# A verdict in five steps, two split loads and a new written order in a gated attention and SoLU kernel

## The chip, the core and the metric

The kernel runs on one core of a Trainium2 chip. Its engines work side by side, each through its own queue in order: TensorE (PE, with its weight loads shown apart as PEld), VectorE (DVE), ScalarE (ACT), GpSimd (POOL) and SyncE (SP), which here issues nearly all DMA transfers. The metric is the time of one execution on the device in microseconds (us). A profile is one execution as the hardware profiler saw it; its span runs from the first to the last instruction.

## The reference

Two blocks follow each other. The first is a gated linear recurrence over 768 time steps, for 4 batches and 8 heads of 48 elements; the gate is complex and its magnitude is clipped:

```python
mag = np.sqrt(a_re * a_re + a_im * a_im)
scale = np.minimum(mag, 0.999) / (mag + 1e-06)
a_re_n, a_im_n = (a_re * scale, a_im * scale)
...
for t in range(S):
    new_re = ar * S_re - ai * S_im
    new_im = ar * S_im + ai * S_re
    S_re, S_im = (new_re + kv, new_im)
    y[:, :, t] = np.einsum('bhd,bhde->bhe', q[:, :, t], S_re)
```

Here kv is the outer product of k and v at step t. Its result, seen as 3072 tokens of 384 values, goes through the second block, with w_in of 384 x 1024 and w_out of 1024 x 384:

```python
h = x @ w_in
e = np.exp(h - h_max)
sm = e / (np.sum(e, axis=-1, keepdims=True) + 1e-09)
solu = h * sm
ln = (solu - mu) / np.sqrt(var + 1e-06) * g_ln
return (ln @ w_out).astype(np.float32)
```

## The kernel before

Time is cut into 6 pieces of 128 steps. A group is one such piece for two batches (12 groups), a chunk is one piece of one batch (24 chunks, two to a group).

For each group the gates are prepared: loads of a_re and a_im (`load_ar`, `load_ai`), then a chain of element operations on ACT and DVE in turn (`inverse`, `ratio`, `sure`, `tangent`, `square`, `secant`, `fourth`, `size`, `eps`, `lnm`) that ends in the logarithm of the magnitude. `total0` and `total1` are its running sums over time, as products on PE with a triangular matrix (L838, one for each batch); `grow` and `decay` take exponentials of them, `angle` and `phase` do the same for the argument, `nearest`, `part`, `cos` and `sin` give the rotations. `trig` and `exp` are loads of ACT's function tables (L933, L936). `qs` and `ks` scale q and k. For group 0 alone the chain is cut in two halves, batch 0 (steps ending in a) and batch 1 (ending in b), though a_re and a_im arrive as one tile for both.

For each chunk `k2` and `q2` build doubled rows on DVE (L947), which are transposed, for chunks 0 and 1 on PE (`qt`, `kt`, copied by ACT as `qT`, `kT`), for the others by DVE and four DMAs (`kqb`, `kqt0`; L956, L961). `score0` and `score1` are products (L1001), `mask0` multiplies by the causal mask on DVE (L1006), `values` is the product with v and the carried state (L1034), `carry` and `add` renew the state (L1042).

The second block follows chunk by chunk: `turned_x` (ACT copy), `up0` and `up1` (PE, f_h, L1075), `exp0` (ACT, f_z), `solu0` (DVE), a transpose (`zt`, `zT` by PE and ACT for chunks 0, 1, 2 and 23, `blocks` and `away` by DVE and four DMAs for the others), `centred`, `spread` and `norm` for the variance, `down0` and `down1` (PE, f_o, L1152), `scale` (ACT, L1156) into f_ot, a pool of two buffers, and `store` (L1161).

The weights are stored as 64-bit numbers. `fetch` brings one of 14 pieces (pieces 0 to 5 of w_in, 6 to 13 of w_out) into a pool of six buffers (f_raw), `raised` (ACT, L736) and `convert` (DVE, three operations, L742 to L746) turn it into 32-bit numbers. `mean`, `meansum` and `centre` take a weighted column mean from w_out. The kernel relies on its inputs lying in certain ranges: extremes are noted along the way (`seen`, `rows`, `sums`), and near the end the 14 pieces are fetched again (`again`) and examined (`inspect`, L749, into `least`). The verdict (L1180 to L1195) counts all of these into one flag. All queues load the flag (L1261), and if it is not zero a slower general program runs (L1262); with these inputs it does not.

The order of all instructions is written out by hand in the list `ORDER`: steps are issued in its order, each engine works through its own share, and waits follow from the data. A step such as `up0:22` is `up0` of chunk 22, for prep steps the number is that of the group, for weight steps that of the piece. Behind the list the code calls the verdict:

```python
for s in ORDER.split():
    nm, i = s.split(":")
    go(nm, int(i))
go("verdict", 0)
```

A buffer of a pool goes to the next tile once the readers of its old tile are done.

Of the kernel before, what the change touches and what calls it, by code (L numbers as in the profile page):

```python
# [19 lines left out]
P = 128  # L20
# [495 lines left out]
load_ar:0 inverseb:0 load_ai:0 ratiob:0 inversea:0 ratioa:0 sureb:0 surea:0 fetch:10 raised:10 tangentb:0 squareb:0  # L516
load_q:0 fetch:1 tangenta:0 squarea:0 secantb:0 secanta:0 sizeb:0 fourthb:0 sizea:0 epsb:0 convert:10 fetch:0 epsa:0
load_k:0 lnmb:0 fetch:3 raised:0 lnma:0 total1:0 fourtha:0 total0:0 decay1:0 grow1:0 convert:0 grow0:0 fetch:4
decay0:0 ks0:0 fetch:11 trig:0 anglea:0 raised:3 load_vr:0 load_ai:1 qs1:0 phase0:0 angleb:0 load_ar:1 nearest0:0
phase1:0 qs0:0 ks1:0 fetch:2 raised:1 convert:3 part0:0 nearest1:0 sina:0 cosa:0 fetch:5 gain:0 convert:1 raised:11  # L520
part1:0 convert:11 raised:4 load_v:0 cosb:0 sinb:0 q2:0 k2:0 fetch:9 fetch:13 q2:1 exp:0 qt1:0 qT1:0 qt0:0 kt1:0 qT0:0
convert:4 inverse:1 kT1:0 kt0:0 score1:0 kT0:0 score0:0 k2:1 onward:0 ratio:1 mask0:0 qt1:1 raised:5 values:0 kt1:1
sure:1 raised:2 qT1:1 fetch:6 tangent:1 square:1 fetch:8 last:0 turned_x:0 kt0:1 convert:2 secant:1 raised:13 kT1:1
convert:5 size:1 convert:13 raised:9 fetch:7 up0:0 eps:1 turn_ends:0 fourth:1 up1:0 raised:6 tot:0 kT0:1 convert:9
lnm:1 exp0:0 fetch:12 raised:7 convert:6 total0:1 carry:1 load_vr:1 total1:1 score1:1 convert:7 grow0:1 decay0:1
solu0:0 decay1:1 grow1:1 trig:1 angle:1 load_q:1 raised:12 load_k:1 qt0:1 ks0:1 phase0:1 qT0:1 phase1:1 nearest1:1
add:1 carry:0 load_ai:2 load_ar:2 nearest0:1 score0:1 convert:12 part1:1 raised:8 part0:1 convert:8 mean:0 mean:4
mean:2 mean:3 qs0:1 sin:1 zt1:0 cos:1 mean:1 mean:6 mask0:1 mean:5 q2:2 k2:2 mean:7 add:0 meansum:0 kqb:2 load_q:2
exp:1 load_q:3 centre:2 values:1 zT1:0 inverse:2 ratio:2 kqt0:2 centre:7 onward:1 turned_x:1 sure:2 centred:0 zt0:0
qs1:1 up1:1 zT0:0 up0:1 last:1 centre:0 tangent:2 score0:2 square:2 score1:2 centre:3 centre:4 secant:2 centre:5 ks1:1  # L530
exp0:1 size:2 load_k:2 centre:1 centre:6 q2:3 eps:2 load_v:1 fourth:2 k2:3 lnm:2 kqb:3 down0:0 turn_ends:1 tot:1
total0:2 spread:0 total1:2 grow1:2 grow0:2 mask0:2 decay0:2 decay1:2 trig:2 solu0:1 down1:0 angle:2 load_ar:3 values:2
kqt0:3 norm:0 scale:0 on:2 load_vr:2 load_ai:3 zt0:1 turned_x:2 zt1:1 carry:2 qs0:2 zT0:1 zT1:1 centred:1 phase0:2
qs1:2 phase1:2 ks1:2 score1:3 load_v:2 score0:3 up1:2 nearest0:2 nearest1:2 ks0:2 part0:2 load_v:4 part1:2 sin:2 add:2
cos:2 up0:2 mask0:3 q2:4 k2:4 exp:2 values:3 down0:1 kqb:4 inverse:3 spread:1 down1:1 turned_x:3 ratio:3 exp0:2 sure:3
solu0:2 kqt0:4 tangent:3 square:3 zt1:2 zt0:2 norm:1 last:2 zT1:2 zT0:2 up1:3 secant:3 size:3 carry:3 load_k:3
score1:4 load_ar:4 k2:5 eps:3 up0:3 scale:1 q2:5 centred:2 exp0:3 lnm:3 score0:4 total0:3 total1:3 kqb:5 load_q:4
fourth:3 grow1:3 decay0:3 kqt0:5 add:3 grow0:3 decay1:3 onward:2 mask0:4 down0:2 store:0 trig:3 solu0:3 angle:3 on:3
centred:3 down1:2 spread:2 values:4 blocks:3 turn_ends:2 last:3 tot:2 turned_x:4 load_ai:4 phase0:3 phase1:3 carry:4
qs0:3 nearest0:3 ks1:3 nearest1:3 ks0:3 part1:3 away:3 store:1 score1:5 norm:2 part0:3 sin:3 cos:3 scale:2 score0:5  # L540
qs1:3 exp:3 up1:4 inverse:4 mask0:5 add:4 up0:4 exp0:4 k2:6 spread:3 q2:6 kqb:6 values:5 ratio:4 load_v:3 sure:4
turned_x:5 solu0:4 down0:3 tangent:4 again:12 turn_ends:3 blocks:4 down1:3 norm:3 square:4 carry:5 kqt0:6 up0:5 up1:5
secant:4 load_vr:3 away:4 q2:7 score1:6 scale:3 size:4 k2:7 eps:4 lnm:4 score0:6 tot:3 total0:4 kqb:7 fourth:4 store:3
total1:4 down0:4 add:5 grow0:4 decay1:4 onward:3 centred:4 exp0:5 spread:4 down1:4 decay0:4 grow1:4 trig:4 load_k:4
mask0:6 angle:4 kqt0:7 values:6 solu0:5 blocks:5 turned_x:6 last:4 on:4 store:2 phase0:4 away:5 phase1:4 load_ar:5
score0:7 carry:6 nearest1:4 ks0:4 nearest0:4 norm:4 qs0:4 centred:5 part1:4 score1:7 part0:4 sin:4 cos:4 add:6 scale:4
# [51 lines left out]
centred:22 store:20 blocks:22 up0:23 scale:21 up1:23 spread:22 away:22 again:2 inspect:5 exp0:23 norm:22 inspect:3  # L598
down0:22 again:0 down1:22 solu0:23 inspect:9 centred:23 scale:22 again:11 again:6 zt0:23 zT0:23 inspect:0 inspect:6
zt1:23 again:4 again:8 store:22 spread:23 inspect:2 store:21 down0:23 norm:23 inspect:8 again:1 zT1:23 down1:23  # L600
inspect:11 inspect:4 scale:23 store:23 inspect:1
"""


# [690 lines left out]
```

## Time and profile before

| | |
|---|---|
| median of 4 runs | 433.65 us (433.12 to 434.98) |
| the profiled execution's own time | 434.3 us |
| its span | 432.4 us |
| mean granted TensorE clock | 0.985 |
| PE, DVE, ACT, POOL busy | 89%, 78%, 67%, 13% of the span |
| bytes read from HBM, written | 38.87 MB, 4.72 MB |

The span is shorter than the time, since it leaves out what lies before the first and behind the last instruction. Busy shares are averages over stages with different limits: the opening (the first 85 us or so), a long middle in which the work of one group repeats, and the end.

The DMA work of SP shows in the list of issues (out<-in, engine, count, size, median us from issue to landing):

```profile
f_kqT<-f_kb SPq DMA_DIRECT2D x88, 192.0 KB, 3.4
f_zT<-f_zb SPq DMA_DIRECT2D x80, 128.0 KB, 3.5
f_raw<-in_moe_w_out_dram SPq DMA_DIRECT2D x16, 384.0 KB, 5.3
f_raw<-in_moe_w_in_dram SPq DMA_DIRECT2D x12, 512.0 KB, 5.5
f_ar<-in_a_re_dram SPq DMA_DIRECT2D x12, 384.0 KB, 5.0
```

f_raw has 28 rows for 14 pieces because of the second fetch.

### The profile page before, as it was taken

To read this page: it belongs to the slowest core of one execution; us is meant where nothing else is said; L and a number is where in the kernel's file an instruction comes from. 1 tells how busy PE (TensorE), PEld (TensorE's weight loads), DVE (VectorE), ACT (ScalarE), POOL (GpSimd) and SP (SyncE) were. 2 spreads that over 40 slices of the span, in tenths; PEclk is the share of its full clock that TensorE was granted. 3 is DMA by queue.
4 is the path that set the end of the run, shared out by engine and by line. 5 is a ranking of instruction groups with operands and counts; after the bars stand their busy time and mean duration, and the time that the engine had idled before them with its cause. 6 is when DMAs were issued, how large, how long until landed. Compare 5 with 4: busy or idle time off the path is not lost.

```text
span 432.4 us, 15839 instructions
## 1 busy us (share of the span) xinstructions
PE 387.0 (89%) x6928; PEld 207.7 (48%) x6928; DVE 335.6 (78%) x457; ACT 288.0 (67%) x475; POOL 57.7 (13%) x139
## 2 busy tenths in 40 slices
PE   0258687999999999999999999999999999999990
PEld 0025243555644544554654555655645545556450
DVE  3788988987797798599789689689788887872352
ACT  4987957896685776678656768766866867522240
POOL 3000100321320110120111010201102102110110
PEclk9999969999999999999999999999999999999997
DMA  9994958588677877668779858869869858579770
GB/s 196 273 232 155 193 81 158 112 144 161 145 167 158 184 147 142 159 145 163 178 145 205 177 112 180 193 128 206 183 150 190 157 137 194 116 168 273 239 239 28
DMA packets 168094, 72.59 MB, mean 168 GB/s; under 512 B 142544, under 2 KB 155856, under 8 KB 168016
## 3 DMA queue, kind: packets, MB, share of 16 engines
q1 hardware_dynamic: 167872, 71.17, 75.2%
q8 instruction: 56, 0.92, 0.9%
q10 hardware_dynamic: 144, 0.33, 0.3%
q14 instruction: 22, 0.18, 0.1%
HBM read 38.87 MB, written 4.72 MB: 101 GB/s over the span
## 4 chain that ended last, share of the span: by engine, by line
PE 74%; DVE 9%; ACT 7%; DMA 3%; issue 3%; SPq 2%; DVEq 0%; ACTq 0%
PE f_o L1152 25%; PE f_h L1075 23%; PE f_y L1034 8%; PE f_score L1001 6%; PE f_phase L838 3%; PE f_L L838 3%; PE f_d L1042 3%; DMA f_ar<-in_a_re_dram 1%; DMA f_raw<-in_moe_w_in_dram 1%; PE f_parts L760 1%; DMA out_dram<-f_ot 1%; DVE f_kb L956 1%; DVE f_kq L947 1%; DVE f_att L1006 1%; DVE f_w_out L770 1%
## 5 line engine op out<-in xcount | busy, mean ns | idle before, releaser
L1152 PE MATMUL f_o<-f_w_out,f_zT 128*32 128x384 f32 (+1 forms) x1344 | 130.2, 487 | 2.7 <-DVE f_w_out L770 1.6
L1075 PE MATMUL f_h<-f_w_in,f_xT 128*32 128x512 f32 x1152 | 130.5, 593 | 1.6 <-ACT f_xT L1068 1.6
L1152 PEld LDWEIGHTS f_o<-f_w_out,f_zT 128*32 128x32 f32 (+1 forms) x1344 | 57.6, 114 | 64.7 <-issue 44.1
L1075 PEld LDWEIGHTS f_h<-f_w_in,f_xT 128*32 128x32 f32 x1152 | 40.9, 110 | 66.4 <-issue 62.8
L956 DVE STREAM_TRANSPOSE f_kb<-f_kq 128x1536 f32<-128x1536 f32 x22 | 56.0, 2544 | 2.7 <-DMA f_kqT<-f_kb 2.5
L1085 ACT ACTIVATE f_z<-f_h 128x1024 f32<-128x1024 f32 x24 | 28.7, 1196 | 20.2 <-PE f_h L1075 20.2
L1094 DVE SCALAR_TENSOR_TENSOR f_z<-f_h,f_z 128x1024 f32<-128x1024 f32 (+1 forms) x36 | 33.4, 955 | 10.1 <-ACT f_z L1085 10.1
L1001 PEld LDWEIGHTS f_score<-f_kqT 96*32 96x32 f32 x1536 | 33.9, 113 | 10.8 <-issue 9.1
L1034 PE MATMUL f_y<-f_att,f_v 128*32 128x128 f32 (+1 forms) x384 | 37.0, 273 | 0.3 <-DVE f_att L1006 0.3
L1034 PE MATMUL f_y<-f_att,f_vr 128*32 128x128 f32 x384 | 36.5, 273 | 0.0
L1001 PE MATMUL f_score<-f_kqT 96*32 96x64 f32 (+3 forms) x1536 | 34.8, 240 | 1.3 <-ACT f_kqT L974 1.0
L1139 POOL TENSOR_SCALAR f_s<-f_s,f_sum 128x1 f32<-128x1 f32 x24 | 12.6, 527 | 174.2 <-ACT f_z L1133 174.0
L838 PE MATMUL f_L<-f_lr,f_mats 128*32 128x384 f32 x192 | 19.3, 517 | 17.4 <-DVE f_lr L833 17.4
L1034 PE MATMUL f_y<-f_kqT,f_state 96*32 96x128 f32 (+1 forms) x640 | 33.9, 272 | 0.0
L1006 DVE TENSOR_TENSOR f_att<-f_score,f_mats 128x1024 f32<-128x1024 f32 x24 | 29.1, 1213 | 5.3 <-PE f_score L1001 5.3
L893 DVE SCALAR_TENSOR_TENSOR f_f<-f_f,f_phase 128x384 f32<-128x384 f32 x24 | 12.9, 554 | 21.4 <-ACT f_f L889 21.1
L1133 ACT ACTIVATE f_z<-f_z,f_less 128x1024 f32<-128x1024 f32 x24 | 27.4, 1142 | 0.0
L1130 POOL TENSOR_SCALAR f_less<-f_sum 128x1 f32<-128x1 f32 x24 | 10.8, 449 | 123.5 <-DVE f_z L1094 123.0
L947 DVE TENSOR_TENSOR f_kq<-f_cs,f_q 128x768 f32<-128x768 f32 x24 | 22.8, 951 | 5.3 <-ACT f_cs L902 4.0
L1156 ACT ACTIVATE f_ot<-f_o,f_rs 128x384 f32<-128x384 f32 x24 | 13.7, 570 | 19.0 <-PE f_o L1152 13.5
L1068 ACT COPY f_xT<-f_y 128x384 f32<-128x384 f32 x24 | 11.3, 470 | 22.6 <-PE f_y L1034 22.6
L1034 PEld LDWEIGHTS f_y<-f_att,f_v 128*32 128x32 f32 (+1 forms) x384 | 22.6, 103 | 7.5 <-issue 4.7
(101 smaller groups left out, 613.6 us busy)
## 6 DMA issues: line engine op xcount, KB each, us to landing
f_kqT<-f_kb SPq DMA_DIRECT2D x88, 192.0 KB, 3.4
f_zT<-f_zb SPq DMA_DIRECT2D x80, 128.0 KB, 3.5
f_raw<-in_moe_w_out_dram SPq DMA_DIRECT2D x16, 384.0 KB, 5.3
f_raw<-in_moe_w_in_dram SPq DMA_DIRECT2D x12, 512.0 KB, 5.5
f_ar<-in_a_re_dram SPq DMA_DIRECT2D x12, 384.0 KB, 5.0
f_ai<-in_a_im_dram SPq DMA_DIRECT2D x12, 384.0 KB, 6.4
f_q<-in_q_dram SPq DMA_DIRECT2D x12, 384.0 KB, 5.3
f_k<-in_k_dram SPq DMA_DIRECT2D x12, 384.0 KB, 5.1
```

What stands on the lines that cost most here:

```text
L838: nc.tensor.matmul(out=ps[r:r + 32], lhsT=weights[:, r:r + 32], rhs=st[nm][:, i * DM:(i + 1) * DM], start=True, stop=True)
L947: nc.vector.tensor_tensor(out=t, in0=T["cs", g][:, i * H:(i + 1) * H], in1=heads(T[nm, g][:, i]).unsqueeze(2).to_broadcast([P, H, 2, D]), ...
L956: nc.vector.transpose(out=t, in_=T["kq", c].rearrange("p n h (f j) -> p j (n h) f", j=3))
L1001: nc.tensor.matmul(out=scores[r0:r0 + 32, x, r:], lhsT=QK[:, r // 32, x], rhs=QK[:, r // 32:, H + x], start=True, stop=True)
L1006: nc.vector.tensor_tensor(out=st["att"].rearrange("p (i u) t -> p i u t", u=2), in0=scores.rearrange("p (i u) t -> p i u t", u=2), in1=mat ...
L1034: nc.tensor.matmul(**product)
L1075: nc.tensor.matmul(out=st["h"][r:r + 32, half * 512:(half + 1) * 512], lhsT=st["xT"][:, c * P + r:c * P + r + 32], rhs=w_in[:, c, half * 5 ...
L1085: nc.scalar.activation(out=z, in_=h, func=AF.Exp, accum_out=sums[:, n:n + 1])
L1094: nc.vector.scalar_tensor_tensor(out=z, in0=h, scalar=1.0, in1=z, op0=OP.mult, op1=OP.mult, accum_out=st["sum"][:, 2 + i:3 + i])
L1133: nc.scalar.activation(out=st["z"], in_=st["z"], func=AF.Square, bias=st["less"], accum_out=st["sum"][:, 1:2])
L1152: nc.tensor.matmul(out=st["o"][rows], lhsT=zT, rhs=w_out[:, c], start=(c == 0), stop=(c == KF - 1))
L1156: nc.scalar.activation(out=st["out"], in_=st["o"], func=AF.Copy, scale=st["rs"])
```

## The change

It has three parts. a_re and a_im of group 0 are loaded by batch, in four loads of 192 KB (`load_arb`, `load_aib`, `load_ara`, `load_aia`), so that each half of the chain depends on its own two. The verdict is cut into `judge`, `judgew`, `judges`, `count` and `flag`, which have places of their own in the list; the scratch tile for the ends of the decays now comes from the weight pieces' pool instead of the second block's. And the list is new from beginning to end. No other operation is added or left out.

```diff
+        def load_one(nm, src, pl, i):
+            def f():
+                if (nm, g) not in T:
+                    T[nm, g] = pl.tile([P, GB, DM], FP, tag=nm, name=f"f_{nm}")
+                nc.sync.dma_start(out=heads(T[nm, g][:, i]), in_=src[b0 + i, :, ti * P:(ti + 1) * P, :].rearrange("h t d -> t h d"))
+            return f
...
+        if g == 0:
+            for nm, src, pl in (("ar", a_re, ld), ("ai", a_im, ld)):
+                del own["load_" + nm]
+                for i in range(GB):
+                    own[f"load_{nm}{'ab'[i]}"] = load_one(nm, src, pl, i)
...
-    def verdict():
+    def judge():
         good = sml.tile([P, 2, NG + 1], FP, tag="good", name="f_good")
-        ends = ffp.tile([P, FF], FP, tag="z", name="f_ends")[0:GH, 0:NG * D].rearrange("p (g d) -> p g d", d=D)
+        ends = rawp.tile([P, 512, 2], I32, tag="raw", name="f_ends").bitcast(FP).rearrange("p n u -> p (n u)")
+        ends = ends[0:GH, 0:NG * D].rearrange("p (g d) -> p g d", d=D)
...
+    def judge_weights():
+        fine = sml.tile([P, 14], FP, tag="fine", name="f_fine")
+        nc.vector.tensor_scalar(out=fine, in0=least, scalar1=TINY, scalar2=None, op0=OP.is_ge)
+        nc.vector.tensor_reduce(out=one_row()[:, 2:3], in_=fine, op=OP.add, axis=AX.X)
...
+    def count():
+        ps = T["count"] = ps_t.tile([P, 512], FP, tag="t", name="f_count")
+        nc.tensor.matmul(out=ps[0:1, 0:4], lhsT=ones[:, 0:1], rhs=T["row"], start=True, stop=True)
...
-    steps["verdict", 0] = verdict
+    steps["judge", 0], steps["judgew", 0], steps["judges", 0] = judge, judge_weights, judge_sums
+    steps["count", 0], steps["flag", 0] = count, verdict
...
-    go("verdict", 0)
```

The list begins and ends, before (-) and after (+), as follows; lines of it that the prediction's steps lie in are among them:

```diff
-load_ar:0 inverseb:0 load_ai:0 ratiob:0 inversea:0 ratioa:0 sureb:0 surea:0 fetch:10 raised:10 tangentb:0 squareb:0
-load_q:0 fetch:1 tangenta:0 squarea:0 secantb:0 secanta:0 sizeb:0 fourthb:0 sizea:0 epsb:0 convert:10 fetch:0 epsa:0
-load_k:0 lnmb:0 fetch:3 raised:0 lnma:0 total1:0 fourtha:0 total0:0 decay1:0 grow1:0 convert:0 grow0:0 fetch:4
...
-inspect:11 inspect:4 scale:23 store:23 inspect:1
+load_arb:0 load_aib:0 inverseb:0 load_ara:0 load_aia:0 fetch:0 ratiob:0 sureb:0 tangentb:0 squareb:0 fetch:10
+secantb:0 sizeb:0 inversea:0 epsb:0 fetch:1 ratioa:0 surea:0 tangenta:0 fourthb:0 squarea:0 secanta:0 lnmb:0 raised:10
+fetch:4 sizea:0 convert:10 epsa:0 raised:1 lnma:0 convert:1 total1:0 load_vr:0 raised:0 grow1:0 fetch:3 total0:0
+load_q:0 convert:0 fourtha:0 decay1:0 grow0:0 decay0:0 trig:0 anglea:0 raised:3 load_k:0 fetch:2 qs1:0 angleb:0
+raised:4 phase0:0 nearest0:0 phase1:0 convert:3 ks1:0 nearest1:0 part0:0 sina:0 ks0:0 load_ar:1 cosa:0 load_ai:1 qs0:0
+fetch:5 part1:0 sinb:0 fetch:11 convert:4 k2:0 q2:0 cosb:0 exp:0 k2:1 fetch:9 qt0:0 fetch:7 inverse:1 qT0:0 kt0:0
...
+mean:0 mean:3 score0:1 mean:4 convert:8 mean:2 mask0:1 cos:1 sin:1 mean:1 add:1 mean:6 mean:7 mean:5 exp:1 load_ar:2
+load_ai:2 centred:0 meansum:0 k2:2 values:1 q2:2 load_k:4 inverse:2 zT1:0 centre:0 kqb:2 load_q:2 ratio:2 zt0:0
...
+values:10 phase0:6 phase1:6 last:6 store:6 store:7 blocks:9 ks1:6 qs0:6 turned_x:10 nearest0:6 carry:10 nearest1:6
...
+inspect:10 inspect:7 centred:23 again:4 inspect:6 zt0:23 inspect:12 judges:0 zt1:23 scale:22 again:1 zT0:23
```

The new list ends with `down1:23 inspect:4 norm:23 inspect:1 judgew:0 count:0 flag:0 scale:23 store:23`.

## The prediction

> **What bounds the kernel now.** I read the page's engine totals and 40 slices first, then busy time by stretches, then the timelines of the two ends.
>
> ```profile
> span 432.4 us, 15839 instructions
> ...
> PE 387.0 (89%) x6928; PEld 207.7 (48%) x6928; DVE 335.6 (78%) x457; ACT 288.0 (67%) x475; POOL 57.7 (13%) x139
> ...
> PE   0258687999999999999999999999999999999990
> ```
>
> The digits are tenths of a slice of 10.8 us. PE is full from the eighth slice to the last but one. The stretches say where its 45.4 idle us (432.4 - 387.0) lie (columns: stretch, its length, busy PE, PEld, DVE, ACT, POOL with counts, granted clock, DMA share, GB/s):
>
> ```profile
> 0.00:15.80 15.80, 0.01 (x3) 0.02 (x3) 7.36 (x22) 9.47 (x20) 3.48 (x11) 1.00 1.01 219
> 15.80:29.10 13.30, 5.56 (x32) 1.07 (x32) 11.07 (x21) 11.81 (x24) 0.00 (x0) 1.00 1.00 251
> ...
> 75.00:85.00 10.00, 9.41 (x93) 5.32 (x96) 9.72 (x16) 8.99 (x18) 2.24 (x5) 1.00 0.64 116
> 85.00:415.00 330.00, 328.44 (x6244) 177.41 (x6239) 260.76 (x312) 219.66 (x356) 48.56 (x113) 1.00 0.77 170
> ...
> 422.40:432.40 10.00, 0.19 (x2) 0.11 (x2) 2.42 (x14) 0.58 (x1) 0.00 (x0) 0.70 0.09 30
> ```
>
> From 85 to 415 us PE is idle for 1.6 us, DVE and ACT for 69 and 110: this part is bound by matmul work that no line of the diff alters. Before 85 us PE is idle for 33.7, and after its last product (422.4) the span runs on for 10.0. So only the two ends can move much. The opening, from the timeline:
>
> ```profile
> 0.72 0.45 SPq L694 DMA_DIRECT2D f_ar<-in_a_re_dram  x1
> ...
> 5.89 0.52 ACT L798 ACTIVATE f_lr<-f_ar 128x384 f32<-128x384 f32 x1 [3.89 <-DMA f_ar<-in_a_re_dram]
> ...
> 7.99 0.56 DVE L804 TENSOR_TENSOR f_ai<-f_ai,f_x 128x384 f32<-128x384 f32 x1 [5.64 <-ACT f_x L799]
> ```
>
> ACT waits 3.89 us for the whole of f_ar. DVE's row names ACT, but that operand was ready at 6.97 (6.45 + 0.52); f_ai, issued at 1.22 and landing 6.7 later (7.92), came last. The end:
>
> ```profile
> 417.33 0.44 SPq L729 DMA_DIRECT2D f_raw<-in_moe_w_in_dram  x1
> ...
> 422.28 0.69 DVE L749 TENSOR_REDUCE f_least<-f_raw 128x1 f32<-128x512 f32 x1 [1.09 <-DMA f_raw<-in_moe_w_in_dram]
> ...
> 422.88 0.17 DVE L1180 TENSOR_SCALAR f_good<-f_seen 128x13 f32<-128x13 f32 x1
> ...
> 424.23 0.16 DVE L1189 TENSOR_SCALAR f_fine<-f_least 128x14 f32<-128x14 f32 x1
> ...
> 425.15 0.14 DVE L1195 TENSOR_SCALAR flag<-f_total 1x1 int32<-1x1 f32 x1
> ```
>
> The last weight piece is fetched at 417.33, inspected at 422.28, and only then do the verdict's ten small DVE operations run, one behind the other. All queues load the flag at 425.3 and branch at 425.9 to 426.0; PE's branch takes 3.68 us (to 429.7), SP's chain is free at 429.4, and the closing barrier ends at 432.4: 7.1 us behind the flag, whatever came before.
>
> **The end, term by term.** After the last inspect the new order leaves two DVE operations (fine and its sum), the product, its sum and the compare: 1.06 us by the old rows (424.23 to 425.29). The other eight (422.88 to 424.23, 1.35 us) move ahead into time in which DVE waits: it idles 2.39 and 1.09 us for the last pieces. The f_ends scratch takes a weight buffer whose reader is an inspect well before it, so it waits for nothing new. The last fetch is placed behind chunk 22's scale in the list, and on SP ahead of the last two stores. It needs the eighth inspect, which I put at 416.1 (the end of the last f_z product, 415.0, plus two inspects of 0.55): 1.2 us before 417.33. With the same 4.93 us it lands at about 421.1; two inspects later DVE is free at 421.9, before PE ends the last f_o (422.33). The count product stands behind that f_o on PE: 422.35 + 0.19, sum and compare (0.33 with the hop): flag at about 422.95 instead of 425.29. Then SP is last: it issues the final store at 423.11 to 423.44 (its place is fixed by PE's end and the scale of 0.58), loads the flag at 423.5 and not 425.3, and its branch (3.5) ends at 427.6 instead of 429.4; PE's ends at 427.2. Gain 1.8 by SP and 2.1 by the barrier's last comer (429.7 to 427.6); I take **1.9**. Bounds: 1.0, if the last inspect stays where it is (422.97 + 1.06 + 0.05 = 424.1, 1.2 earlier), and 2.35, the flag's whole lead. The final store's landing (3.6 median for its kind) ends before 427.6 and stays hidden; if it took the 8.6 of the slowest, the end would come at 431.7 + about 2.7.
>
> **The opening, term by term.** Two loads of 384 KB become four of 192 KB, batch 1 first. No row shows such a half. Bounds for its landing behind the issue: 3.4 us (f_kqT, 192 KB, longer runs) and 5.15 (the whole f_ar). The queue is in order, so half the bytes should come roughly a microsecond sooner: I take 4.15, landing at 4.9; the others at about 5.9, 6.9 and, as before, 7.9. The two extra issues cost SP 0.45 each while the queue is full anyway (the second load's issue already takes 2.40). Then I walked the new written order by the old durations (ACT 0.52 and 0.56 to a dependent successor, 0.71 with an accumulator read; DVE 0.56; a w_out convert 1.59, a w_in convert 1.9; 1.57 from a running sum's first product to its reader), each step at the later of its operands and its engine's previous step:
>
> - first running-sum product 13.5 (was 15.79), because one half goes through to lnm by itself;
> - trig table 19.3 (19.59): the lead is used up, as three raised pieces instead of two stand before it on ACT;
> - exp table 27.25 (28.61), first product ratio of group 1 at 30.8 (33.32), as the sines of both halves are no longer spread between raised steps;
> - mask of chunk 0 at 35.6 (36.27), exp of chunk 0 at 45.5 (46.56), mask of chunk 1 at 57.1 (58.31);
> - copy of the column means 61.3 (63.08): the exp table now loads before it, in time in which ACT waited 4.27 us for f_parts;
> - last centre of w_out 72.1 (75.4), phase of group 2 on PE 83.95 (85.43), with the same products done by then.
>
> So **1.5**, of which the moved steps keep most and the split loads about 0.3 (the trig row). The walk counts waits that I saw and none that I missed, so I take 1.2. Bounds: a loss of 1.0 and a gain of 2.6 (the lead at ratio of group 1). What it pays: q stood behind one weight piece and k behind three, now both stand behind five and v's reversed rows. With mats, 4.2 MB go to the end of q and 4.6 to that of k; by 219 GB/s to 15.8 us (3.46 MB), 251 from there and 1 us to landing, q is in at about 19.8 and k at 21.3. Their readers on DVE come at 20.4 and 22.8 in my walk; behind them stand a convert and the part step. The cover is thus 0.6 and 1.5 us, and each microsecond beyond is one lost. Reversed v and v (in at about 35) are needed at 36.9.
>
> The granted clock enters here: it is 0.53 in 54 to 60 us, and eight f_parts products take 2.74 us there against about 1.4 later (1.48 at 61.55). In my walk PE has like gaps (49.3 to 52.0), so I leave this stretch where it is.
>
> [...]
>
> **The loop**, 85 to 415 us: the same products in almost the same PE order, DVE and ACT with 20% and 33% of slack. Its 1.6 idle us may vanish or double; I take 0, bounds -1.5 and +1.5.
>
> Sum: 432.4 - 1.9 - 1.2 = 429.3 us of span. The profiled execution itself took 434.3, the median of the four runs is 433.65, 1.25 above the span; I carry 1.25 over: **430.6**.
>
> **Rivals.**
> 1. *The halves gain nothing and the walk's lead melts.* For it: the lead is only 0.3 us at the trig table, DMA share is 1.01 and 1.00 in the first two stretches, q's cover is 0.6. Against: the lead comes back at three later rows by moves that don't touch loads. Then 432.4 - 1.9 + 1.25 = 431.75.
> [...]
> 2. *PE keeps its clock, or fills its gaps better*: f_parts at full clock is worth 1.3 us and lies on the way to the centres. 430.6 - 1.3 - 0.7 = 428.6.
> 3. *Stores stall the loop* (slower). The new order puts two stores side by side at six places (chunks 6 to 17), just ahead of the scale that needs their f_ot buffer, and the next f_o needs that scale to free PSUM. Between, PE has about 9.1 us of other work (values 0.9, phase 1.3, d 0.65, h 5.2, score 1.1). It decides when a store is issued more than 4.9 us after the end of f_o (9.1 less a landing of 3.6 and a scale of 0.57). The old order has it once: a store at 228.87 lands 4.09 later and PE loses 1.08 us in that stretch (200 to 240). Against: SP's other loads are spread. Six times 0.8 to 1.1 is 4.8 to 6.6: 435.4 to 437.2.
> 4. *The tail does not shorten* (the last fetch or inspect is late, or the barrier waits for something else): 432.4 - 1.2 + 1.25 = 432.45. If moreover nothing of the opening holds, the change does not do what it says: 433.65.
>
> **How the numbers follow.** Forecast 0.50 (own range 429.3 to 432.0), rivals 0.18, 0.10, 0.14 and 0.08. Low end: 430.6 - 1.4 (opening at 2.6) - 0.45 (tail at 2.35) - 1.5 (loop) = 427.25. The high end reaches 435.0 and so cuts into the third rival. A change of 0.3% (1.3 us) is about what this measurement can tell from none: faster is below 432.35, slower above 434.95. Faster: 0.48 + 0.13 + 0.10 = 0.71; slower: the third rival and a little of the first, 0.16; the rest 0.13.
>
> **What would show it.** Right: first inverse near 4.9; first f_L product near 13.5; exp table near 27.3; last centre before 74; flag within 1 us of PE's last f_o; 9 us or less from there to the end. Wrong: DVE waiting for q or k near 20 us, a clock of 0.5 over f_h or f_o, f_ot waiting for stores after 200 us, or an inspect ending behind PE.

## The result, and the profile after

The changed kernel takes 433.88 us (median of 52 executions, 430.9 to 437.7), the kernel before on the same chip 434.39 us (78 executions, 430.3 to 438.1). The ratio is 0.9988, 95% interval 0.9974 to 1.0002: half a microsecond less, which cannot be told from no change. The forecast was 3.05 us less. The four runs shown before (433.65) lie 0.7 below the median of the 78, and single executions of one kernel spread over nearly 8 us, so that one profile is a sample: the profiled execution of the changed kernel has a longer span than the one of before.

```profile
span 433.1 us, 15841 instructions
...
PE 386.1 (89%) x6928; PEld 216.0 (50%) x6928; DVE 334.3 (77%) x457; ACT 289.2 (67%) x475; POOL 54.5 (13%) x139
...
PE   0358697899999999999999999999999999999991
```

That is the page of the changed kernel; PE's slices have the same shape. From the timeline, ACT's first step and then PE from the first f_o to the first phase product of group 2 (start, length, engine, line, what it writes and reads, idle time before it and what ended that):

```profile
4.84 0.52 ACT L812 ACTIVATE f_lr<-f_ar 128x384 f32<-128x384 f32 x1 [2.83 <-DMA f_ar<-in_a_re_dram]
```

```profile
70.78 4.51 PE L1166 MATMUL f_o<-f_w_out,f_zT 128*128 128x384 f32 x8 [2.22 <-DVE f_w_out L784]
75.22 1.33 PE L1015 MATMUL f_score<-f_kqT 96*32 96x128 f32 x64
76.36 0.84 PE L852 MATMUL f_L<-f_lr,f_mats 128*32 128x384 f32 x8
77.14 2.85 PE L1166 MATMUL f_o<-f_w_out,f_zT 128*128 128x384 f32 x8
79.91 0.85 PE L852 MATMUL f_L<-f_lr,f_mats 128*32 128x384 f32 x8
...
84.28 0.88 PE L1056 MATMUL f_d<-f_v,f_kq 128*32 128x48 f32 x48 [1.62 <-ACT f_xT L1082]
84.98 1.50 PE L852 MATMUL f_phase<-f_x,f_mats 128*32 128x384 f32 x16
```

The same stretch of PE in the profile of before:

```profile
72.67 1.31 PE L1001 MATMUL f_score<-f_kqT 96*32 96x128 f32 x64
75.55 2.82 PE L1152 MATMUL f_o<-f_w_out,f_zT 128*128 128x384 f32 x8 [1.57 <-DVE f_w_out L770]
78.47 1.50 PE L838 MATMUL f_L<-f_lr,f_mats 128*32 128x384 f32 x16
79.90 2.85 PE L1152 MATMUL f_o<-f_w_out,f_zT 128*128 128x384 f32 x8
...
85.43 0.51 PE L838 MATMUL f_phase<-f_x,f_mats 128*32 128x384 f32 x1
```

The first inverse is 1.05 us earlier than before (4.84, was 5.89), and the first f_o starts 4.8 us earlier (70.78, was 75.55). At the phase product 0.45 us is left of it (84.98, was 85.43). In between stand a first f_o of 4.51 us instead of 2.82, the score products of chunk 2 behind it, a running sum (f_L, 79.91) behind the second half of f_o, and 1.62 us in which PE waits for ACT. Busy times of five stretches (stretch, length, busy PE, PEld, DVE, ACT, POOL with counts, granted clock, DMA share, GB/s):

```profile
68.28:71.69 3.41, 1.19 (x7) 0.68 (x4) 3.41 (x7) 1.73 (x4) 0.00 (x0) 1.00 0.58 112
71.69:75.10 3.41, 3.41 (x6) 1.35 (x5) 3.41 (x5) 3.38 (x3) 0.00 (x0) 0.50 1.00 195
75.10:85.00 9.90, 8.28 (x180) 5.38 (x180) 6.69 (x13) 7.18 (x15) 1.66 (x6) 1.00 0.46 105
85.00:415.00 330.00, 327.73 (x6204) 186.33 (x6199) 257.44 (x305) 220.24 (x356) 45.92 (x111) 1.00 0.78 168
423.40:433.10 9.70, 0.19 (x2) 0.11 (x2) 0.46 (x3) 0.58 (x1) 0.00 (x0) 0.67 0.10 31
```

The clock is 0.50 just where the long f_o lies. The loop leaves PE idle for 2.27 us (was 1.56). The end, from the timeline:

```profile
422.49 0.69 DVE L763 TENSOR_REDUCE f_least<-f_raw 128x1 f32<-128x512 f32 x1 [0.58 <-DMA f_raw<-in_moe_w_in_dram]
422.56 0.81 PE L1166 MATMUL f_o<-f_w_out,f_zT 128*128 128x384 f32 x2
423.21 0.17 DVE L1207 TENSOR_SCALAR f_fine<-f_least 128x14 f32<-128x14 f32 x1
...
423.73 0.19 PE L1218 MATMUL f_count<-f_row,f_mats 128*1 128x4 f32 x2 [0.36 <-DVE f_row L1208]
423.96 0.15 DVE L1222 TENSOR_REDUCE f_total<-f_count 1x1 f32<-1x4 f32 x1 [0.37 <-PE f_count L1218]
...
424.14 0.14 DVE L1223 TENSOR_SCALAR flag<-f_total 1x1 int32<-1x1 f32 x1
```

PE is done at 423.37 and the flag at 424.28: 0.91 us behind it, where it was 2.97. So the verdict's steps did move into DVE's waiting time. But the span ends 8.85 us behind the flag, where it was 7.12. What SP does there, register, branch and semaphore instructions, is in the trace and in no line of the page; the table below e5_pad and e9_before_pad counts it.

### The profile page after: what moved, and what is told of

Same layout as the page of the kernel before. It is cut to its first block, busy times and chain, and to the rows that moved or that the text cites. A ratio compares the mean times of both kernels' runs of the same rounds, so it can differ in the third digit from the quotient of the medians.

```text
span 433.1 us, 15841 instructions
## 1 busy us (share of the span) xinstructions
PE 386.1 (89%) x6928; PEld 216.0 (50%) x6928; DVE 334.3 (77%) x457; ACT 289.2 (67%) x475; POOL 54.5 (13%) x139
## 4 chain that ended last, share of the span: by engine, by line
PE 65%; DVE 10%; DMA 8%; ACT 7%; SPq 4%; issue 3%; DVEq 0%; ACTq 0%
PE f_h L1089 22%; PE f_o L1166 21%; PE f_y L1048 7%; PE f_score L1015 5%; PE f_phase L852 3%; DMA f_v<-in_v_dram 3%; PE f_d L1056 3%; PE f_L L852 2%; SPq L1131 2%; DMA f_ai<-in_a_im_dram 2%; DMA f_raw<-in_moe_w_in_dram 1%; DVE f_kb L970 1%; DVE f_kq L961 1%; ACT f_z L1099 1%; ACT L947 1%
## 5 line engine op out<-in xcount | busy, mean ns | idle before, releaser
L1166 PE MATMUL f_o<-f_w_out,f_zT 128*32 128x384 f32 (+1 forms) x1344 | 131.9, 488 | 2.5 <-DVE f_w_out L784 2.2
L1166 PEld LDWEIGHTS f_o<-f_w_out,f_zT 128*32 128x32 f32 (+1 forms) x1344 | 62.0, 114 | 62.0 <-issue 40.1
L1089 PEld LDWEIGHTS f_h<-f_w_in,f_xT 128*32 128x32 f32 x1152 | 45.9, 110 | 61.6 <-issue 55.8
L970 DVE STREAM_TRANSPOSE f_kb<-f_kq 128x1536 f32<-128x1536 f32 x22 | 54.0, 2456 | 2.3 <-DMA f_kqT<-f_kb 2.0
L1015 PE MATMUL f_score<-f_kqT 96*32 96x96 f32 (+3 forms) x1536 | 35.0, 236 | 1.0 <-issue 1.0
L1020 DVE TENSOR_TENSOR f_att<-f_score,f_mats 128x1024 f32<-128x1024 f32 x24 | 29.1, 1214 | 6.1 <-PE f_score L1015 6.1
L852 PE MATMUL f_phase<-f_x,f_mats 128*32 128x384 f32 x192 | 21.0, 546 | 5.2 <-ACT f_x L890 5.2
L961 DVE TENSOR_TENSOR f_kq<-f_cs,f_k 128x768 f32<-128x768 f32 x24 | 22.8, 950 | 3.4 <-ACT f_cs L919 2.4
L1126 DVE STREAM_TRANSPOSE f_zb<-f_z 128x1024 f32<-128x1024 f32 x20 | 24.7, 1233 | 0.1
L1048 PEld LDWEIGHTS f_y<-f_att,f_vr 128*32 128x32 f32 x384 | 23.8, 109 | 1.5 <-issue 1.2
```

Of the source, the lines that this page charges most:

```text
L852: nc.tensor.matmul(out=ps[r:r + 32], lhsT=weights[:, r:r + 32], rhs=st[nm][:, i * DM:(i + 1) * DM], start=True, stop=True)
L961: nc.vector.tensor_tensor(out=t, in0=T["cs", g][:, i * H:(i + 1) * H], in1=heads(T[nm, g][:, i]).unsqueeze(2).to_broadcast([P, H, 2, D]), ...
L970: nc.vector.transpose(out=t, in_=T["kq", c].rearrange("p n h (f j) -> p j (n h) f", j=3))
L1015: nc.tensor.matmul(out=scores[r0:r0 + 32, x, r:], lhsT=QK[:, r // 32, x], rhs=QK[:, r // 32:, H + x], start=True, stop=True)
L1020: nc.vector.tensor_tensor(out=st["att"].rearrange("p (i u) t -> p i u t", u=2), in0=scores.rearrange("p (i u) t -> p i u t", u=2), in1=mat ...
L1048: nc.tensor.matmul(**product)
```

## The experiments

Every kernel was compared with the kernel before on its own chip. Where two edited kernels of one chip are compared, the interval comes from resampling their executions.

**e1_tail, e2_no_tail: the two ends apart.** In e1 the list of before runs up to the second fetch of piece 13 (an earlier second fetch, of piece 12, moves behind that point), then the rest in the new order; in e2 the other way round:

```diff
 score0:22 score1:22 kqt0:23 down0:20
-again:13 blocks:21 mask0:22 centred:20 inspect:12 again:3 down1:20
+again:8 centred:20 again:9 spread:20 inspect:8 again:0 mask0:22 again:7
```

```diff
 cos:11 centred:19 sin:11 exp:11 q2:22
-again:8 ks0:11 values:21 down0:19
+again:12 last:10 ks0:11 k2:22 spread:19
```

> The kernel before, with whole loads of a_re and a_im and its own order up to the second fetch of piece 13; from there on the order of the changed kernel, with the verdict in five steps. Theory A (the earlier flag is worth what the prediction said, and it was the opening that was lost): PE's last f_o ends near 422.3, the flag is ready within 1.0 us of it instead of 2.96, the end comes 7 to 7.5 us behind the flag, the time is 1.5 to 2.1 us below before, a ratio of 0.995 to 0.9965. Theory B (the new end costs PE a part of it, since inspects and fetches now lie beside the exponential and the SoLU product of chunk 23, and PE's last f_o ended 1.05 us later in the changed kernel): last f_o 0.7 to 1.1 us later than before, flag 1 us earlier, time 0.7 to 1.2 us below before, ratio 0.997 to 0.9985. Theory C (what follows the flag takes the gain back): flag 1 to 2 us earlier, end 8.5 us or more behind it, ratio 0.999 to 1.001.

e1: 438.57 us, ratio 1.0087 (1.0048 to 1.0126). None of the theories; the seam is at fault. DVE's timeline:

```profile
391.75 0.55 DVE L761 TENSOR_REDUCE f_least<-f_raw 128x1 f32<-128x384 f32 x1 [5.99 <-DMA f_raw<-in_moe_w_out_dram]
392.23 1.22 DVE L1018 TENSOR_TENSOR f_att<-f_score,f_mats 128x1024 f32<-128x1024 f32 x1
```

An inspect stands ahead of the mask of chunk 22, its piece was fetched only just before, and DVE waits 5.99 us in the loop, PE 4.35 behind it. As to the end it still has a row: flag 0.64 us behind PE's last f_o, end 8.95 behind the flag.

> The changed kernel (split loads and the new order) up to where the weight pieces are fetched the second time, then the order of before, with all five parts of the verdict in one block at the end as before. What the opening and the loop give by themselves. Theory A (the lead of the opening is gone before the loop: half a clock for the first f_o, and a running sum put behind the second half of f_o): first phase product of group 2 near 85, 0.2 to 0.7 us ahead of before, the end as in before, ratio 0.998 to 1.001. Theory B (the opening's lead survives, the tail is worth nothing): ratio 0.996 to 0.998. Theory C (the new loop order is worse): first phase product at 85, but PE idle for 1 us or more beyond the 1.6 of before between 85 and 400, ratio 1.000 to 1.003.

e2: 434.57 us, 1.0015 (0.9977 to 1.0053); phase product at 84.47, PE idle for 2.39 us in the loop. That lies between theories A and C: opening and loop alone gain nothing. The end was not as in before, as the expectation has it: the flag came 3.82 us behind PE's last f_o and the end 11.79 (before: 2.97 and 10.09). But that f_o itself ended at 423.24, later than in both profiles of before (422.32 and 421.11).

**e3_scores: three steps moved back.**

```diff
+score1:2 score0:2
 down0:0 eps:2 add:0 exp0:1 q2:3 lnm:2 spread:0
-score1:2 score0:2
 fourth:2 total1:2 kqb:3 mask0:2 norm:0 grow1:2
+total0:2
 down1:0 load_k:3 decay1:2
-total0:2
```

> The changed kernel with three steps moved: the two score products of chunk 2 ahead of the first half of the first f_o, and the second running sum of group 2 ahead of its second half, as the order before had them. Theory A (PE's idle 2.2 us before the first f_o puts the clock to one half for 3.4 us, and the sum's place makes the trig table wait): PE idle before that f_o at most 1.6 us, f_o 2.8 to 3.0 us instead of 4.5, trig table of group 2 at 79.5 to 80.5 instead of 81.7, first phase product of group 2 at 83.0 to 84.0 instead of 85.0, time 1.0 to 1.8 us below the changed kernel, ratio to before 0.995 to 0.9965. Theory B (the phase product hangs on something else, DVE or the transfers, so that the moves change nothing behind it): phase product 84.5 to 85.2, ratio as that of the changed kernel, 0.998 to 1.0.

432.01 us, 0.9949 (0.9921 to 0.9977), 1.7 us below the changed kernel by the ratios, with an interval of some 1.4 on either side. PE's timeline:

```profile
71.07 1.33 PE L1014 MATMUL f_score<-f_kqT 96*32 96x128 f32 x64 [1.68 <-DMA f_kqT<-f_kb]
72.34 2.85 PE L1165 MATMUL f_o<-f_w_out,f_zT 128*128 128x384 f32 x8
75.79 1.50 PE L851 MATMUL f_L<-f_lr,f_mats 128*32 128x384 f32 x16 [0.61 <-DVE f_lr L846]
77.22 2.85 PE L1165 MATMUL f_o<-f_w_out,f_zT 128*128 128x384 f32 x8
...
83.30 1.50 PE L851 MATMUL f_phase<-f_x,f_mats 128*32 128x384 f32 x16
```

Both running sums now run ahead of the second f_o, and the phase product comes at 83.30, 1.0 to 1.7 us ahead of the changed list's (84.32 to 84.98 in after, e2 and e5). Theory A, with one reserve: an f_o of 2.85 us does not come from the edit alone, as e2 and e5 have 2.82.

**e4_fill: useless products in PE's gap.**

```diff
+    def fill():
+        ps = ps_t.tile([P, 512], FP, tag="t", name="f_fill")
+        for _ in range(4):
+            nc.tensor.matmul(out=ps, lhsT=ident, rhs=w_in[:, 0, 0:512], start=True, stop=True)
```

> The changed kernel with four products of 128x512 that nobody reads put on PE just ahead of the first f_o, where it sat idle for 2.2 us: added work and nothing else. Theory A (the clock is lowered by the idle time): the four take about 1.9 us and fit into the gap, no half clock at 71.7 to 75.1, the first f_o takes 2.8 to 3.0 us instead of 4.5, the second running sum of group 2 starts 1.2 to 1.7 us earlier (78.2 to 78.7), time 0.5 to 1.5 us below the changed kernel. Theory B (the first f_o is slow for another reason, such as its operand being written just before): f_o still 4.3 to 4.7, time as the changed kernel or up to 0.3 us above.

434.31 us, 0.9990 (0.9955 to 1.0026): as the changed kernel.

```profile
69.68 3.70 PE L1218 MATMUL f_fill<-f_w_in,f_mats 128*128 128x512 f32 x8
73.21 2.74 PE L1165 MATMUL f_o<-f_w_out,f_zT 128*128 128x384 f32 x8
```

The four took 3.70 us, twice what was expected, and pushed f_o back by about what they saved. f_o took 2.74 us here, but e2 and e5 have 2.82 without any filler. Nothing is settled by e4.

**e5_pad, e9_before_pad: idle instructions on SP.** In the first six profiles SP stands still once behind the branch, and the place moves with the length of SP's program.

```diff
+    def pad():
+        for _ in range(24):
+            nc.sync.drain()
...
+pad:0
 load_ar:6
```

> The changed kernel with 24 instructions that do nothing (drains) put into SP's queue in the middle of the loop, ahead of a load of a_re. In the profiles so far SP stands still once behind the branch at the end, 1.04 us in before and 1.95 to 2.33 us in the others, after its 16th, 17th, 13th, 19th, 17th and 17th instruction (before, after, e1, e2, e3, e4); the instructions of SP's program and that place add up to 746 each time where the count is known (730, 729, 733, 727, 729). Theory A (SP runs to the end of a block of code there and waits for the next one, and this is what took back the earlier flag): the branch now goes 7 instructions beyond that place, no standstill, the end comes 6.5 to 7.0 us behind the flag instead of 8.85, the time is 1.5 to 2.2 us below the changed kernel, ratio to before 0.9940 to 0.9960. Theory B (SP waits for a transfer or for another engine): the standstill stays at 1.9 to 2.1 us, or goes over to another engine; ratio 0.998 to 1.0.

> The kernel before with the same 24 idle instructions in SP's queue ahead of the same load. Theory A (the standstill behind the branch is its own cost, 1.04 and 0.84 us in the two profiles of before): it goes, the end comes 5.9 to 6.3 us behind the flag instead of 7.12 and 6.69, time 0.7 to 1.2 us below before, ratio 0.997 to 0.9985; then the changed kernel is ahead of it by 2.0 to 2.6 us once both are rid of the standstill. Theory B (the 24 instructions help for another reason, by the same 3 us as in e5_pad): ratio 0.991 to 0.994.

e5: 431.29 us, 0.9912 (0.9888 to 0.9937), 3.3 us below the changed kernel by the ratios, more than the 2.05 us of the standstill, with an interval of about 1.2 on either side. e9: 433.24 us, 0.9980 (0.9947 to 1.0014), 0.9 below before by the ratio. Neither shows a standstill on SP:

```profile
L1318 SPq DRAIN  x3: 7/13/130, 430.2 to 432.6; - x3
L1322 SPq DRAIN  x3: 7/7/7, 429.3 to 429.7; - x3
```

These are SP's last three drains in after and in e5 (count, shortest, median and longest in ns, first and last start): 2.4 us apart in the one, with the standstill behind the first of them, 0.4 in the other. Theory A is nearer in both, though e5 gained more than its range and e9's end is 6.52 us behind its flag instead of 5.9 to 6.3: the same 24 instructions are worth much to the changed kernel and little to the other. For every profile (SP's instructions in the program, with the general part that is skipped; from the trace, the one behind the branch after which SP stands still, for how long; from PE's last f_o to the flag, from the flag to the end):

```
                 SP   after  stands  f_o-flag  flag-end
before          730    16     1.04     2.97      7.12
e8 (= before)   730    16     0.84     2.91      6.69
after           729    17     2.05     0.91      8.85
e1_tail         733    13     2.33     0.64      8.95
e2_no_tail      727    19     1.97     3.82      7.97
e3_scores       729    17     1.95     0.91      8.68
e4_fill         729    17     1.95     0.72      8.88
e6_verdict      730    16     2.03     2.59      8.60
e5_pad          753     -      -       0.63      7.05
e7_scores_pad   753     -      -       0.91      8.06
e9_before_pad   754     -      -       2.95      6.52
e10_pads        753     -      -       0.91      6.40
e11_whole_pad   750     -      -       2.25      7.94
e12_loop        755     -      -       0.94      6.63
e13_both_pads   753     -      -       0.75      6.55
e14_whole_pads  750     -      -       3.01      6.62
e15_before_pads 754     -      -       3.02      6.41
```

The first two columns add up to 746 in all eight rows that have a place, and with 24 more instructions no standstill is left. The standstills lie between 4.4 and 7.2 us behind the branch. From 4.17 to 5.73 us behind it in after, and from 4.03 to 5.90 in before, the queues that the page calls "instruction" move packets of 8 and 16 KB, as they do at some other times behind it. That SP comes to the end of a block of code there and waits for the next one (theory A) is the author's reading: it goes with the fixed place, but no record ties a packet to the wait, and no run shows what SP waits for. SP's first instruction behind the branch starts 3.41 us behind it in before and 3.93 in after.

**e6_verdict: the verdict alone,** the list of before otherwise:

```diff
-zT1:23 down1:23 inspect:11 inspect:4 scale:23 store:23 inspect:1
+zT1:23 down1:23 judge:0 judges:0 inspect:11 inspect:4 inspect:1 judgew:0 count:0 flag:0 scale:23 store:23
```

> The kernel before with whole loads, its own order and its own second fetches and inspects; only the verdict is cut into its five steps: the parts on the extremes and the sums ahead of the last three inspects, the rest behind them, and the last scale and store behind the compare. PE's last f_o should end near 422.3 and the last inspect near 423.0 as before. Theory A (the flag sets the end): flag 1.0 to 1.4 us earlier than before (3.0 behind PE's last f_o then, 1.6 to 2.0 now), time 0.9 to 1.4 us lower, ratio 0.9967 to 0.998. Theory B (SP's standstill behind the branch is 2 us in all kernels but the one profile of before, and takes the gain back): the flag as in A, the end 8 us or more behind it, ratio 0.999 to 1.001.

433.87 us, 0.9967 (0.9941 to 0.9993). The time is at the edge of theory A. The profile shows theory B's row, a standstill of 2.03 us and the end 8.60 behind the flag, and a flag 2.59 behind PE's last f_o, where both theories had 1.6 to 2.0. This run decides nothing.

**e7_scores_pad, e10_pads, e12_loop: both cures together, ACT's queue too, and the old loop.** e7 is e3 and e5 together; e10 adds to it

```diff
+        for _ in range(8):
+            nc.scalar.drain()
```

and e12 puts the loop of before into e10.

> The changed kernel with both edits: the three steps of e3_scores moved in the opening, and the 24 idle instructions on SP. If both theories hold, the gains add up: 1.7 us by the opening and 1.5 to 2.0 by the end, phase of group 2 on PE at 83 to 84, end 6.5 to 7.0 us behind the flag, ratio to before 0.990 to 0.993. If SP's standstill is no cost of its own: as e3_scores, 0.994 to 0.996.

> e7_scores_pad with eight more idle instructions (drains), on ACT's queue. In the profile of e7_scores_pad ACT's last instruction came 1.5 us behind those of the other engines (8.95 against 7.43 us behind PE's last f_o), behind its fourth instruction after the branch; in e2_no_tail ACT stood still 2.45 us behind its second; with ACT's 1222 and 1224 instructions both give 1226, as SP's places gave 746. Theory A (the same code boundary on ACT): no engine is late at the end, end 6.4 to 7.1 us behind the flag instead of 8.06, time 0.5 to 1.5 us below e7_scores_pad, ratio to before 0.987 to 0.9895. Theory B (ACT's lateness was this one execution, as e5_pad with the same count did not show it): ratio as e7_scores_pad, 0.989 to 0.992.

> e10_pads with the loop in the order of before (from a little ahead of the first phase product of group 2 to the doubled rows of chunk 20, some 84 to 350 us), opening and end as in e10_pads. From the first phase product of group 2 to PE's last f_o the profiles of before, e8 and e6 have 336.9, 337.2 and 337.7 us, those of after, e2 and e5 338.4, 338.8 and 338.2. Theory A (the new order of the loop costs about 1 us): this stretch takes 336.8 to 337.8 us, time 0.7 to 1.5 us below e10_pads, ratio to before 0.984 to 0.987. Theory B (the difference is made at the end, where inspects and fetches lie beside chunk 23, or is scatter): the stretch takes 337.9 to 338.8 us, time within 0.5 us of e10_pads.

e7: 430.73 us, 0.9898 (0.9850 to 0.9946), within 0.6 us of e5 (interval -2.8 to 1.6), phase product at 83.26. So the gain of the opening is there. The end, 8.06 us behind the flag, lacks part of the other, as ACT's last instruction comes 1.5 us behind all others. The time cannot tell whether the gains add up. e10: 429.89 us, 0.9862 (0.9811 to 0.9913), end 6.40 behind the flag. It has the lowest median of all and beats both kernels (6 executions). For ACT the evidence is thinner than for SP: e7 and e11 stand still behind the fourth instruction, e5 with as many instructions does not, and of e2's 2.45 us some 0.9 lie behind the moment at which the other engines went on. e12: 431.44 us, 0.9915 (0.9883 to 0.9948), 1.6 above e10 (interval -0.4 to 3.7). From the phase product to PE's last f_o it took 338.6 us; that is in theory B's range, though e10 itself took 340.4 there. By the times theory A falls: the old loop is not faster.

**e8_before: a second profile of before.**

> The kernel before, unchanged, for a second profile of the same program. Theory A (the short standstill of SP behind the branch, 1.04 us, belongs to the program): again 0.9 to 1.3 us, end 7.0 to 7.3 us behind the flag. Theory B (it was this one execution): 1.8 to 2.4 us, end 8 us or more behind the flag. The half clock, 54.4 to 61.2 us in the first profile: if its windows are laid by a clock that does not know where a program starts, it comes at another place or length; if it is the program's, at the same one within 1 us.

432.59 us (one execution). The standstill of 0.84 and the end 6.69 behind the flag lie just below theory A's ranges and far from theory B's: this program has the short one. The phase product of group 2 came at 83.90, not at 85.43. And the half clock lay at 52.70 to 59.53 instead of 54.40 to 61.22, 1.70 us apart in the same program: by the expectation's test the place is not the program's. Another stretch lies from 21.98 to 32.22, where the first profile has no clock record (its records begin at 37.33).

**e11_whole_pad, e13_both_pads, e14_whole_pads, e15_before_pads: halves or whole loads, with the ends made equal.** e11 and e14 have

```diff
-load_arb:0 load_aib:0 inverseb:0 load_ara:0 load_aia:0 fetch:0
+load_ar:0 load_ai:0 inverseb:0 fetch:0
```

e13, e14 and e15 have both sets of idle instructions; e13 is the changed kernel with them, e15 the kernel before.

> The changed kernel with a_re and a_im of group 0 loaded whole again (two loads of 384 KB instead of four of 192 KB), and the 24 idle instructions of e5_pad, so that it stands against e5_pad. Theory A (the halves bring the first running sum forward, but nothing that lasts): first f_L 15.0 to 15.8 instead of 13.6, first phase product of group 2 within 0.4 us of e5_pad's 84.3, time within 0.6 us of e5_pad's, ratio 0.9900 to 0.9930. Theory B (the lead of the halves lives on to the loop): phase of group 2 at 85.0 to 86.0, time 0.8 to 1.8 us above e5_pad, ratio 0.993 to 0.996.

> The changed kernel, 24 idle instructions on SP and 8 on ACT, nothing moved. Theory A (the code boundaries took back the earlier flag, the rest of the forecast held in the main): end 6.4 to 7.1 us behind the flag, ratio to before 0.988 to 0.992, and 2.0 to 3.5 us below e15_before_pads. Theory B (the opening's part of the forecast, 1.2 us, was never there, and the tail's part was): 1.2 to 2.0 us below e15_before_pads, ratio 0.992 to 0.995.

> As e13_both_pads with whole loads of a_re and a_im. Theory A (e11_whole_pad was slow by ACT's standstill and a late inspect, the halves are worth no more than the 0.3 us of the prediction): within 0.6 us of e13_both_pads. Theory B (the new order, without the halves, runs 1.6 us late at the first phase product of group 2, 85.9 instead of 84.3 us, and keeps that to the end): 1.0 to 2.2 us above e13_both_pads.

> The kernel before, 24 idle instructions on SP and 8 on ACT. ACT's program is already beyond its boundary there (1229 instructions against 1226), so that the 8 should change nothing. Theory A: as e9_before_pad, ratio to before 0.996 to 0.9995, end 5.9 to 6.6 us behind the flag. Theory B (idle instructions on ACT help by themselves): ratio below 0.995.

e11: 434.69 us, 0.9996 (0.9965 to 1.0028), phase product at 85.89 as theory B has it, but with ACT standing still for 2.04 us and the flag 2.25 behind PE's last f_o. e13: 431.16 us, 0.9936 (0.9905 to 0.9967). e14: 433.73 us, 0.9965 (0.9934 to 0.9996), some 2.5 above e13 by the medians (0.2 to 3.8), 1.3 by the ratios. First f_L 15.92 instead of 13.78, phase product 86.83 instead of 85.30. Theory B is nearer, though the interval does not exclude A, and the flag, 3.01 behind PE's last f_o instead of 0.75, adds to the difference. e15: 433.34 us, 0.9986 (0.9953 to 1.0019), as e9: ACT's idle instructions do nothing there. e13 is 2.2 us below e15 (0.6 to 4.3): that is what the change is worth where no engine stands still behind the branch. By the distance to e15 it is theory A for e13, by the ratio to before theory B, and the intervals exclude neither.

## Why the prediction was wrong

**The tail: the flag came as forecast, and one sentence on what follows it was wrong.** The flag was to come within 1 us of PE's last f_o: 0.91 (0.63 to 0.94 in the eight kernels that have the new end and the split loads). The end was to come 9 us or less behind that f_o: 9.76. The step that failed is "the closing barrier ends at 432.4: 7.1 us behind the flag, whatever came before". It came 8.85 behind it, and it does depend on what came before: the place where SP stands still behind the branch moves with the length of its program (the two add up to 746 in all eight profiles with a standstill), and in the nine with 24 idle instructions there is none. The profile of before had it too: SP is not free at 429.4, but stands still from 430.46 to 431.48, ahead of the barrier. From PE's last f_o to the end it took 10.09 and 9.60 us in the two profiles of before, and 9.76, 9.60, 9.60 and 9.59 in after, e1, e3 and e4: instead of the 1.9 us taken, some 0.2 was gained. Without standstills it is 9.47 and 9.43 (e9, e15) against 7.68, 7.30, 7.57 and 7.30 (e5, e10, e12, e13), about 2.0. The prediction's fourth rival ("the barrier waits for something else"), with its second sentence ("nothing of the opening holds"), is what happened; it had 0.08. Why the standstill is 1 us in the program of before and 2 in the others, e6 with the same place among them, stays open: in both profiles of before SP was the first engine to resume behind the branch, in after and e6 it was not, and that is all they show.

**The opening: right as far as the last centre, and then not.** The walk's rows against the trace: first inverse 4.9 and 4.84, first f_L 13.5 and 13.66, trig table 19.3 and 19.54, exp table 27.25 and 27.52, ratio of group 1 30.8 and 30.73, mask of chunk 0 35.6 and 35.46, its exponential 45.5 and 45.49, mask of chunk 1 57.1 and 57.90, copy of the means 61.3 and 59.39, last centre 72.1 and 70.64. q and k arrived in time (20.67 and 23.03, no wait). The step that failed is the last: "phase of group 2 on PE 83.95 (85.43), with the same products done by then". It came at 84.98, and at 84.47, 84.32 and 85.30 in e2, e5 and e13 with the same opening. With the list of before up to there, six profiles (before, e8, e1, e6, e9, e15) have 85.43, 83.90, 84.45, 83.86, 84.84 and 83.72. So the means are 84.8 and 84.4, and the profile that the prediction went by was the latest of six: of 1.2 us nothing was gained. By PE's last f_o it is no better: 422.5 us on average in these four, 421.4 in the five of the old list without e1, whose loop was disturbed.

The lead of 3 us at the last centre is lost behind it: from there to the phase product it took 10.0 to 10.1 us in all six, 12.7 (e2, e5) and 14.3 (after, e13) with the new list; the 1.6 between the latter lie mostly in the first f_o (in after 4.51 us, in e2 and e5 2.82). The second running sum stands behind down1 in the list, so the trig table and the copy that f_d needs come late (1.62 us of waiting, 1.23 in e2 and e5), and the score products, which before ran ahead of the first f_o, run behind it, while PE waits 2.2 to 2.5 us instead of 1.57. e3 moved these three steps: its phase product came at 83.30, and its time was 1.7 us lower.

**The split loads.** "About 0.3 of it" was mis-sized. At the phase product whole loads cost 1.5 us (e14, 86.83, against e13, 85.30) and 1.6 (e11, 85.89, against e5, 84.32); there the new order without halves is behind the old one (84.4). The 2.5 us of time between e14 and e13 are not all of this kind. In e14 the last inspect starts 1.21 us behind PE's last f_o, in e13 1.05 ahead of it, and the end comes 9.6 behind it instead of 7.3. Why the last pieces land late in e14 and e11 stays open; e1, with whole loads and the old loop, has its flag 0.64 behind PE's last f_o.

**The clock.** "I leave this stretch where it is", said of PE's gaps (49.3 to 52.0 in the walk; the longest ahead of the stretch in before 2.25 us, to 52.79), missed that a second one could come; a clock of 0.5 over f_o was one of the prediction's signs of being wrong. In after the first f_o took 4.51 us, with a clock of 0.50 from 71.69 to 75.10; in e10, e13 and e14 it took 4.2 to 4.5 too, in e2, e3, e5, e7, e11 and e12 2.8 to 2.9 (in e5 at 1.00). The same opening can have either, so for one execution it is scatter. But with the old opening none of six profiles has the long f_o, and with the new one, where e3's three steps stay in their places, three of six have it (after, e13, e14; not e2, e5, e11): on average it is a price of the new order.

By an estimate much of the opening is not at full clock either. The 1.00 that the prediction's table has for its first two stretches (0 to 29.1 us) is no reading: the traces have no clock record before 18.6 to 40.7 us, those of before begin at 37.33, of after at 34.14. In after the first running sum took 1.51 us:

```profile
13.66 1.51 PE L852 MATMUL f_L<-f_lr,f_mats 128*32 128x384 f32 x8 [13.66 <-DMA f_vr<-in_v_dram]
```

Eight products of the same shape take 0.84 us at 76.36, where the granted clock is 1.00. Sixteen phase products take 2.79 us at 21.41, as long as at 51.79, where it is 0.50, and 1.50 at 84.98, where it is 1.00. From these times the half clock of the opening is estimated. In e6, e8 and e15, where the records begin with full clock at 18.6 to 19.1, the score products of chunk 0 took 1.31 us and the phase product of group 2 came at 83.72 to 83.90. In before, e1 and e9 they took 2.34 and it came at 84.45 to 85.43. So the scatter of the base goes with the time of these products and, by the same estimate, with the clock of the opening. With the new list the score products took 2.08 us or more in all eleven profiles; why is not shown.

**The loop.** From the phase product to PE's last f_o: 336.9, 337.2, 337.7, 336.7 and 336.9 us with the old loop (before, e8, e6, e9, e15; mean 337.1), 338.4, 338.8, 338.2, 335.7, 336.8 and 336.4 with the new (after, e2, e5, e13, e11, e14; mean 337.4). "0, bounds -1.5 and +1.5" holds, and the rival of stalling stores didn't show: in the loop of after no f_o product waited at all. The kernels with the edited opening took longer there (e3, e7 and e10: 337.9, 338.3 and 340.4); whether they give back part of their lead was not pursued.

In sum the forecast's 1.9 + 1.2 became about 0.2 in the tail and nothing in the opening. The measured 0.5 +- 0.6 does not contradict that.

## What to carry to other kernels

In this kernel the end did not hang on the last value alone: it came 6.40 to 8.95 us behind the flag. So where a kernel ends in a branch, look at the semaphore and branch instructions behind it. Here SP stood still for 0.84 to 2.33 us at a fixed count of its program, and 24 idle instructions ahead took that away (the 8 on ACT rest on a few profiles). Take the base of a forecast from several executions: rows of one profile moved by up to 1.7 us in the opening, more than the 1.2 us of gain that were forecast there. And follow a lead to the point where it has to arrive; ten steps that came true said nothing of the eleventh, where two steps of the list stood in another order.

## What the hardware showed that was not expected

In the profiles of before and after, every stretch between two changes of the granted clock lasts 3.41 us or a whole number of times that: half clock from 54.40 to 61.22 in before, from 51.21 to 54.62 and from 71.69 to 75.10 in after, full clock from 54.62 to 71.69 in after. Up to 12 us before the end the clock went from full to half three times in these two. In the 3.41 us just ahead PE was busy for 0.45 of the time (before, 50.98 to 54.40), 0.19 and 0.35 (after, 47.80 to 51.21 and 68.28 to 71.69). Cut from the first clock record on into pieces of 3.41 us, the other pieces at full clock have 0.52 or more (0.52 in before, 44.16 to 47.57, and in after, 81.93 to 85.34), and behind them the clock stayed at 1.00. The windows of after above show the last of the three (1.19 of 3.41 us is 0.35, then 0.50). For e5, with 2.48 us of waiting ahead of the same f_o:

```profile
70.42:73.83 3.41, 2.08 (x7) 1.32 (x8) 3.41 (x7) 1.70 (x3) 0.00 (x0) 1.00 0.62 115
73.83:77.25 3.42, 3.42 (x78) 1.98 (x77) 3.42 (x3) 3.42 (x4) 0.00 (x0) 1.00 0.82 159
```

The gap is longer (2.48 us, in after 2.22), but 0.61 of the first stretch is busy, and the clock stays at 1.00. So in these rows it is the busy share of such a stretch that goes with the clock, and not the length of a gap: with 2.2 to 2.5 us of idle time ahead of it the first f_o took 1.4 to 1.7 us more (after, e13, e14) or nothing more (e2, e5, e11).
